# A dilated gated convolution on one core: the first window's loads reordered between queues, the last octet's gate and stores cut into halves and banks

## The chip, the cores and the metric

The kernel runs on 1 core of one Trainium2 chip. Its time is device microseconds of one execution. Five engines take part, each with its own instruction stream: PE (matmuls; its weight loads are listed as PEld), DVE (element-wise on SBUF and PSUM), ACT (element-wise and the tables for tanh and sigmoid), POOL (memsets, masks, and DMAs issued by software) and SP (which here only issues DMAs). DMAs issued by SP travel on queue q1, those issued by ACT on q10, those issued by POOL on q0; all three queues are served by the same 16 DMA engines.

## The reference

```
B, T, D, K = 2, 16000, 144, 15          # x [B,T,D], w [K,D,2D], w_o [D,D], all bf16
xp = pad(x, 28 rows of zeros ahead of each sequence)
h  = sum over i of  xp[:, 28 - 2*i : 28 - 2*i + T, :] @ w[i]
f, g = h[..., :D], h[..., D:]
out = (tanh(f) * sigmoid(g)) @ w_o
```

## The kernel before, in words

**Tiling.** Each sequence of 16000 rows is cut into windows of 2048 rows, 16 windows in all (the last of a sequence overlaps its neighbour, and only its last 104 of 128 row groups are stored). A window holds 16 row phases for 128 row groups; it is worked on as two octets (rho 0 and 1), one for the 8 even phases and one for the 8 odd ones, so there are 32 octets, n = 0 to 31.

**Channels.** 144 channels do not fit 128 partitions. The first 128 arrive by a transposing DMA of x (`load`, L89, tile xn). The other 16, the remainder, are gathered in 32-byte runs (`gather`, L99, tile xt), regrouped by residue on ACT (`rest`, L113) and differenced on DVE (`rest_diff`, L117) into xs, written back to a DRAM scratch xg (`spread`, L123; one DMA for each of the two), and read from there by two more transposing DMAs (`remainder`, L128, tiles rx and re).

**The convolution.** The 15 taps are folded in the manner of a fast convolution: differences of x (`d2`, `d4`, `d8`, `d48`, `d28`, `d24`, `d248`, all DVE at L160) meet sums of the weights. The weight sums are made once at the start: on DVE (`sm`, `ss`, `a1v`, `av`, `bc`, `ev`, L167) and on PE by an identity matrix with an eviction on ACT (`summed`, L235 and L237, called by `raw_sums`, `pair_sums`, `rest_sums`). w arrives in four quarters of its taps (L204); the 16 remainder rows of every tap arrive as `raw` (L206, L207). Each octet has leaves A1, A2, A3, B1, C1, E1 of matmuls into PSUM banks (L302), copies of them on ACT (L331, L335, L366) and combinations on DVE (L369, L387, L392) that end in y. Then tanh and sigmoid on ACT (L397), their product z on DVE (L404), a transposing DMA of z (L408), the output matmul (L434), its cast into the window's tile o (L424 on ACT, L426 on DVE), and one store of a whole window (L450, rows of 4608 bytes).

**What sets the order.** The schedule is manual: every engine runs its instructions in the order in which the program issues them. For octets in the middle this order comes from `PLAN` (L16): each entry is a step and the octet, relative to the running one, that it is done for. The start is written out by hand: fillers of zeros that keep PE busy (`NWARM` matmuls at L186, `keep` at L288), the loads, the weight sums, and the list `first` (L569) for octet 0. The step `wg` is `spread`, `cr` is `rest` and `dr` is `rest_diff`; at L578 those of window 1 are put early, in the place of `wg`, among the first steps of octet 1. The end is written out too: `finish_early` (L520) stands ahead of the product of the last octet's second gate, `finish` (L529) behind it. The last octet's z is transposed on PE (`z_by_pe`, L411) and not by DMA. Octets 29, 30 and 31 are called a, b and c below: a is the second of window 14, b and c are the two of window 15.

**The start before.** SP issues xn(0), w's first and second quarter, the two raw loads, w's third and fourth quarter, then the transposes rx(0), re(0), xn(1) and the gather xt(1). ACT issues xt(0) and the first of the two writes to xg, POOL issues the second one. SP waits, in order, for what each of its DMAs needs.

**The end before.** tanh and sigmoid of c are done as two gates of 576 columns each (k = 0 and 1). Window 15 is stored by two DMAs of whole rows when both b and c are cast: row groups 24 to 63 from SP, 64 to 127 from ACT.

Of the kernel before, what the change touches and what calls it, by code (L numbers as in the profile page):

```python
# [8 lines left out]
BF16 = mybir.dt.bfloat16  # L9
F32 = mybir.dt.float32  # L10
# [16 lines left out]
def kernel(  # L27
# [16 lines left out]
    NWARM = 20  # L44
# [88 lines left out]
    def derive_steps(s):  # L133
        ahead = {"x": 0}

        def sub(name, of, d, first=None, run=0):
# [4 lines left out]
            def go(which=slice(None)):  # L141
                if which.start in (None, 0):
                    s[name] = xd_pool.tile([P, WB], BF16, name=name)
                t, x = s[name], s[of]
                if name == "d4":
                    forms = [((0, [[1, hi]]), (4, [[4, hi // 2], [1, 2]]), (0, [[4, hi // 2], [1, 2]]))]
                elif first is None:
                    forms = [((0, [[1, hi]]), (d, [[1, hi]]), (0, [[1, hi]]))]
# [8 lines left out]
                for form in forms[which]:  # L157
                    o, a, b_ = (bass.AP(t_.tensor, t_[:, c + p:c + p + 1].offset, [t_.ap[0]] + dims)
                                for (c, dims), t_, p in zip(form, (t, x, x), [pad.get(k, 2) for k in (name, of, of)]))
                    nc.vector.tensor_tensor(out=o, in0=a, in1=b_, op=ALU.subtract)  # L160
# [38 lines left out]
    gather(0, nc.scalar)  # L199
# [48 lines left out]
    spread(0, (nc.scalar, nc.gpsimd))  # L248
# [17 lines left out]
    for c in range(4):  # L266
# [4 lines left out]
        if c == 2:  # L271
            pre0["d48"]()
# [72 lines left out]
    class Octet:  # L345
# [48 lines left out]
        def act(self, k, name, lo, func):  # L394
            t = act_pool.tile([P, 4, D], BF16, name=name)
            self.g[name, k] = t
            nc.scalar.activation(out=t[:], in_=self.t["y"][:, k::2, lo:lo + D], func=func)  # L397

        def mult(self, k, part):
            z = self.get(z_pool, "z", [P, 9, CM], BF16)  # L400
            o, lo, n = dict(a=(z[:, k:8:2, :], 0, CM), b=(z[:, 8, :].rearrange("p (r c) -> p r c", c=CR)[:, k::2, :], CM, CR),
                            z=(z[:].rearrange("p g c -> p (g c)").rearrange("p (r c) -> p r c", c=D)[:, k::2, :], 0, D))[part]
            th, sg = self.g["th", k], self.g["sg", k]
            nc.vector.tensor_tensor(out=o, in0=th[:, :, lo:lo + n], in1=sg[:, :, lo:lo + n], op=ALU.mult)  # L404
# [6 lines left out]
    def z_by_pe(o, blocks, by):  # L411

        zt, z = o.get(zt_pool, "zt", [P, 9, P], BF16), o.t["z"]
        for i in range(0, len(blocks), 4):
            b = blocks[i:i + 4]
            ps = bank(True)[:].bitcast(BF16).rearrange("p (g m) -> p g m", m=256)
            for k, g in enumerate(b):
                nc.tensor.transpose(ps[:, k, 0:P], z[:, g, :], ident[:])
            copy_by(by, zt[:, b[0]:b[-1] + 1:2, :], ps[:, 0:len(b), 0:P])
        o.zt = zt  # L420
# [7 lines left out]
    def outproj(o, g, end=False):  # L428
        r0, n = 3 * g, min(3, 8 - 3 * g)
        o.po[g] = bank(False) if end else ps_o.tile([P, 512], F32, name="po", tag="po")  # L430
        if not o.by_phase:
            for c in range(r0, r0 + n + 1):
                a, e = max(c - 1, r0), min(c + 1, r0 + n)
                nc.tensor.matmul(o.po[g][:, (a - r0) * D:(e - r0) * D], lhsT=o.zt[:, c, :],  # L434
                                 rhs=wo_z[:, c, a - c + 1:e - c + 1, :].rearrange("p r e -> p (r e)"), start=c == r0, stop=c == r0 + n,
                                 skip_group_check=True)
            return
        nc.tensor.matmul(o.po[g][:, 0:n * D], lhsT=o.zt[:, 8, :], rhs=wo_bd[:, r0:r0 + n, :].rearrange("p r e -> p (r e)"),  # L438
                         start=True, stop=False)
        for i in range(n):  # L440
            nc.tensor.matmul(o.po[g][:, i * D:(i + 1) * D], lhsT=o.zt[:, r0 + i, :], rhs=wo_m[:], start=False, stop=i == n - 1)  # L441
# [5 lines left out]
    def store(wi, eng, a=0, e=P):  # L447
        b, t0, m0 = wins[wi]
        a = max(a, m0)
        eng.dma_start(out=out[b, t0 + 16 * a:t0 + 16 * e, :].rearrange("(m r) e -> m r e", r=16), in_=outs[wi][a:e, :, :])  # L450
# [7 lines left out]
    def issue(n, name):  # L458
# [38 lines left out]
        elif name[:2] == "th":  # L497
            o.act(int(name[2]), "th", 0, ACT.Tanh)
# [120 lines left out]
```

## Time and profile before

| what | value |
|---|---|
| median of 3 runs | 332.78 us (331.69 to 332.83) |
| the profiled execution's own time | 332.82 us |
| its span in the trace | 330.8 us, so 2.0 us lie around it |
| PE busy | 321.4 us (97%) |
| DVE, ACT busy | 293.5 us (89%), 242.0 us (73%) |
| granted clock | 0.999 |
| last matmul of the convolution starts | 320.67 us |
| last store issued | 326.37 us |

The span is read in three stretches: the start, up to about 24 us, in which loads and waits set the pace; the middle, in which PE is busy nearly all the time; and the end from 320.7 us, in which there is no convolution left and a chain of small steps leads to the last byte stored. In the trace an idle time is shown in brackets with what ended it.

### The profile page before, as it was taken

What the parts mean: (1) busy time and instruction counts of PE and PEld (TensorE: products, weight loads), DVE (VectorE), ACT (ScalarE), POOL (GpSimd) and SP (SyncE); (2) the same over time, 40 slices, a digit from 0 to 9 for tenths busy, and PEclk for the clock granted to TensorE, in tenths of its full rate; (3) what the DMA queues carried; (4) which work ended last, traced back from release to release, by engine and by line L of the source; (5) the groups of instructions that cost most, each with busy time, mean ns of one, the idle gap of its engine ahead of it and who ended that gap; (6) DMA issues with size and microseconds to landing.
All of it is one profiled execution on the core that took longest, in us unless ns stands there. A gap on an engine that the chain in (4) does not pass through costs nothing.

```text
span 330.8 us, 7432 instructions
## 1 busy us (share of the span) xinstructions
PE 321.4 (97%) x2657; PEld 303.1 (92%) x2657; DVE 293.5 (89%) x664; ACT 242.0 (73%) x571; POOL 26.3 (8%) x56
## 2 busy tenths in 40 slices
PE   8899999999999999999999999999999999999993
PEld 3589999999999999999999999999999999999982
DVE  2889999989999998999999899999989999998683
ACT  2737777777877777788777778877777787777763
POOL 5959100000000000000000000000000000000000
PEclk9999999999999999999999999999999999999999
DMA  8779897895949579594979769495986859594113
GB/s 173 160 139 157 155 210 138 151 185 100 206 109 204 151 130 222 77 213 102 175 181 169 157 119 187 109 209 137 145 208 119 171 112 189 154 143 132 38 36 129
DMA packets 194993, 49.64 MB, mean 150 GB/s; under 512 B 190487, under 2 KB 192896, under 8 KB 194957
## 3 DMA queue, kind: packets, MB, share of 16 engines
q1 hardware_dynamic: 188894, 40.07, 69.6%
q10 hardware_dynamic: 4799, 8.58, 7.0%
q0 software_dynamic: 1264, 0.53, 0.9%
q8 instruction: 20, 0.33, 0.4%
q14 instruction: 16, 0.13, 0.1%
HBM read 2.82 MB, written 11.40 MB: 43 GB/s over the span
## 4 chain that ended last, share of the span: by engine, by line
PE 90%; DMA 4%; SPq 2%; DVE 2%; issue 1%; POOL 1%; ACT 0%; DVEq 0%
PE bc L302 56%; PE a L302 25%; PE po L434 9%; DMA xn<-in_x_dram 2%; DMA xt<-in_x_dram 1%; SPq L128 1%; DMA xg<-zero 1%; SPq L89 1%; DVE d L160 0%; DVE o L426 0%; DVE y L392 0%; DVE z L404 0%; POOL xg L123 0%; PE bc L438 0%; PE bc L441 0%
## 5 line engine op out<-in xcount | busy, mean ns | idle before, releaser
L302 PEld LDWEIGHTS <-d 128*128 128x128 bf16 x1792 | 225.4, 145 | 7.8 <-issue 1.4
L302 PE MATMUL bc<-w_all,d 128*128 128x288 bf16 x832 | 140.0, 286 | 0.3 <-DVE t L387 0.3
L392 DVE TENSOR_TENSOR y<-q,bc 128x288 f32<-128x288 f32 x192 | 86.4, 450 | 7.6 <-PE bc L302 5.7
L331 ACT COPY bc<-bc 128x288 f32<-128x288 f32 x97 | 38.5, 397 | 30.1 <-PE bc L302 24.3
L369 DVE TENSOR_TENSOR q<-a1s,a 128x288 f32<-128x288 f32 x126 | 54.2, 451 | 1.5 <-PE a L302 0.8
L424 ACT CAST o<-po 128x432 bf16<-128x432 f32 (+1 forms) x87 | 41.7, 479 | 17.1 <-PE po L434 17.1
L160 DVE TENSOR_TENSOR d<-d 128x516 bf16<-128x516 bf16 (+3 forms) x65 | 52.2, 805 | 0.0
L302 PE MATMUL a<-sm,d 128*128 128x288 bf16 x252 | 50.2, 286 | 0.0
L331 ACT COPY a<-a 128x288 f32<-128x288 f32 x95 | 36.6, 386 | 13.6 <-PE a L302 10.6
L160 DVE TENSOR_TENSOR d<-xn 128x516 bf16<-128x516 bf16 (+2 forms) x48 | 41.1, 859 | 5.1 <-DMA xn<-in_x_dram 5.1
L397 ACT ACTIVATE th<-y 128x576 bf16<-128x576 f32 x64 | 43.9, 685 | 1.1 <-DVE y L392 1.1
L397 ACT ACTIVATE sg<-y 128x576 bf16<-128x576 f32 x64 | 43.7, 683 | 0.0
L434 PE MATMUL po<-wo_z,zt 128*128 128x144 bf16 (+1 forms) x323 | 43.4, 253 | 0.0
L302 PE MATMUL bc<-bc,d 128*128 128x288 bf16 x256 | 41.8, 286 | 0.0
L302 PE MATMUL bc<-wo_p,re 128*128 128x288 bf16 x128 | 36.6, 286 | 0.0
L302 PE MATMUL bc<-we_r,re 128*128 128x288 bf16 x128 | 36.6, 286 | 0.0
L387 DVE TENSOR_TENSOR t<-q,bc 128x288 f32<-128x288 f32 x64 | 28.8, 451 | 8.3 <-PE bc L302 8.3
L434 PEld LDWEIGHTS <-zt 128*128 128x128 bf16 x341 | 29.9, 98 | 4.1
L335 ACT COPY bc<-bc 128x288 f32<-128x288 f32 x64 | 25.0, 393 | 11.2 <-PE bc L302 7.0
L392 DVE TENSOR_TENSOR y<-t,bc 128x288 f32<-128x288 f32 x64 | 26.1, 450 | 5.9 <-PE bc L302 5.9
L404 DVE TENSOR_TENSOR z<-th,sg 128x576 bf16<-128x576 bf16 (+1 forms) x66 | 29.1, 443 | 0.0
L302 PEld LDWEIGHTS <-re 128*128 128x128 bf16 x256 | 28.8, 113 | 0.0
(79 smaller groups left out, 275.5 us busy)
## 6 DMA issues: line engine op xcount, KB each, us to landing
out_dram<-o ACTq DMA_DIRECT2D x13, 576.0 KB
xg<-xs SPq DMA_DIRECT2D x30, 65.0 KB
xt<-in_x_dram SPq DMA_DIRECT2D x13, 71.5 KB
w_all<-in_w_dram SPq DMA_DIRECT2D x3, 288.0 KB
out_dram<-o SPq DMA_DIRECT2D x1, 576.0 KB
zt<-z SPq DMA_TRANSPOSE x31
out_dram<-o ACTq DMA_DIRECT2D x1, 468.0 KB
out_dram<-o ACTq DMA_DIRECT2D x1, 288.0 KB
```

The source lines that it names most:

```text
L89: nc.sync.dma_start_transpose(out=xn[:, lo:WB], in_=src)
L160: nc.vector.tensor_tensor(out=o, in0=a, in1=b_, op=ALU.subtract)
L302: nc.tensor.matmul(ps[:, 0:D2], lhsT=l, rhs=r, start=start, stop=stop, skip_group_check=on)
L331: nc.scalar.copy(out=self.ts[1][:, 0:D2], in_=self.ts[0][:, 0:D2])
L335: nc.scalar.copy(out=self.other[i][:, 0:D2], in_=self.ts[i][:, 0:D2])
L369: nc.vector.tensor_tensor(out=self.get(cp_pool, name, [P, 2, D2], F32)[:, i, :], in0=self.t["a1s"][:, i, :], in1=leaf.ts[i][:, 0:D2], op=op)
L387: nc.vector.tensor_tensor(out=self.get(cp_pool, "t3", [P, 2, D2], F32)[:, i, :], in0=self.t["q3"][:, i, :], in1=self.C1.ts[i][:, 0:D2], op ...
L392: nc.vector.tensor_tensor(out=y[:, k + 4 * i, :], in0=self.t[q][:, i, :], in1=ts[i][:, 0:D2], op=op)
L397: nc.scalar.activation(out=t[:], in_=self.t["y"][:, k::2, lo:lo + D], func=func)
L404: nc.vector.tensor_tensor(out=o, in0=th[:, :, lo:lo + n], in1=sg[:, :, lo:lo + n], op=ALU.mult)
L424: nc.scalar.copy(out=o, in_=a)
L434: nc.tensor.matmul(o.po[g][:, (a - r0) * D:(e - r0) * D], lhsT=o.zt[:, c, :], rhs=wo_z[:, c, a - c + 1:e - c + 1, :].rearrange("p r e -> p ...
```

## The change

It has three parts.

**The start's queues.** xt(0) is issued by SP right behind xn(0), not by ACT. The first write to xg goes to SP too, and stands ahead of the two raw loads and of w's last quarter; w's first three quarters stay ahead of it. SP's order becomes xn(0), xt(0), w in three quarters, xg, raw, raw, w's last quarter, rx(0), re(0), xn(1), xt(1).

**The start's sums.** NWARM falls from 20 to 18, and `keep` from 8 fillers in all to 3. On DVE d2 moves between the first and the second sums, d48 from behind the third to behind the second, and d24, which was done in two halves, is one instruction; d28 comes ahead of the sum bc. On PE the pair sums come in an order that follows w's quarters, and the common part of A3 (`vA3`) comes ahead of A2's private part. `rest` and `rest_diff` of window 1 move behind the step q2_1 of octet 1, with `spread`.

**The end.** c's second gate is done in two halves, k = 1 and k = 3, of 288 columns. `finish_early` and `finish` become one function; c's z is transposed as [0, 2, 4, 6], [1, 5] and [3, 7, 8]; its output matmuls are ordered by when their block arrives. b's half of window 15 is stored as soon as b is cast, and each of c's three banks by a DMA of its own: all of these write runs of 288 bytes, 832 runs for b, 312, 312 and 208 for c.

```diff
-    NWARM = 20
+    NWARM = 18
...
-                    if name == "d24" and s is sets[0]:
-                        forms = [((first, runs), (first, runs), (first + e, runs)), ((first + e, runs), (first + 2 * e, runs), (first + e, runs))]
-                    else:
-                        forms = [[(c, [runs[0], [k, 2], runs[1]]) for c, k in ((first, e), (first, 2 * e), (first + e, 0))]]
+                    form = [(c, [runs[0], [k, 2], runs[1]]) for c, k in ((first, e), (first, 2 * e), (first + e, 0))]
...
-    gather(0, nc.scalar)
+    gather(0)
...
-    for c in range(0, 16, 4):
+
+    def load_w(c):
         nc.sync.dma_start(out=w_all[:, c:min(c + 4, K), :], in_=w[c:min(c + 4, K), 0:CM, :].rearrange("k c d -> c k d"))
-        if c == 4:
-            nc.sync.dma_start(out=raw[:, 0, :], in_=w[0:K:2, CM:D, :])
-            nc.sync.dma_start(out=raw[0:P - CR, 1, :], in_=w[1:K:2, CM:D, :])
+    for c in (0, 4, 8):
+        load_w(c)
...
-    spread(0, (nc.scalar, nc.gpsimd))
+    spread(0, (nc.sync, nc.gpsimd))
+    nc.sync.dma_start(out=raw[:, 0, :], in_=w[0:K:2, CM:D, :])
+    nc.sync.dma_start(out=raw[0:P - CR, 1, :], in_=w[1:K:2, CM:D, :])
+    load_w(12)
...
-        if c == 2:
-            pre0["d48"]()
+        if c < 2:
+            pre0[("d2", "d48")[c]]()
...
+    pair_sums(0)
     raw_sums(0)
+    pair_sums(1)
     rest_sums(slice(0, 3))
-    pair_sums(0)
-    pair_sums(1)
-    keep(5)
-    raw_sums(1, (1,))
+    keep(2)
+    raw_sums(1)
     add(av[:], quad[:, :, 0], quad[:, :, 1])
-    pre0["d2"]()
+    pre0["d28"]()
     add(bc[:, 2:4], wq[:, 2:4, 0], wq[:, 2:4, 1])
-    pre0["d28"]()
-    pre0["d24"](slice(0, 1))
+    pre0["d24"]()
...
+    def outproj_last(o, blocks):
+
+        for c in blocks:
+            g, lo, n, w_ = (c // 3, c % 3, 1, wo_m[:]) if c < 8 else \
+                (c - 8, 0, min(3, 8 - 3 * (c - 8)), wo_bd[:, 3 * c - 24:min(3 * c - 21, 8), :].rearrange("p r e -> p (r e)"))
+            new = g not in o.po
+            if new:
+                o.po[g] = bank(False) if g else ps_o.tile([P, 512], F32, name="po", tag="po")
+            nc.tensor.matmul(o.po[g][:, lo * D:(lo + n) * D], lhsT=o.t["zt"][:, o.at[min(c, 8)], :], rhs=w_, start=new, stop=c >= 8,
+                             skip_group_check=True)
...
+    def store_phases(o, wi, r0, n, eng):
+        b, t0, a = wins[wi]
+        r = o.rho + 2 * r0
+        dst = bass.AP(out.tensor, out[b, t0 + 16 * a + r, 0:1].offset, [[16 * D, P - a], [2 * D, n], [1, D]])
+        eng.dma_start(out=dst, in_=outs[wi][a:P, r:r + 2 * n - 1:2, :])
...
-    def finish_early():
-
-        n = NO - 3
-        for g in range(3):
-            outproj(live[n], g, g > 0)
-        for g, by in ((0, "DVE"), (1, "DVE"), (2, "ACT")):
-            project_out(live[n], window_out(n), g, by)
-        z_by_pe(live[NO - 1], [0, 2, 4, 6], "ACT")
-
...
+        a, b, c = (live[n] for n in range(NO - 3, NO))
+        c.at = {}
+        window_out(NO - 1)
+        for g in range(3):
+            outproj(a, g, g > 0)
+        outproj(b, 0, True)
+        z_by_pe(c, [0, 2, 4, 6], "ACT")
+        c.mult(1, 4)
+        c.mult(3, 4)
+        for g, by in ((0, "ACT"), (1, "DVE"), (2, "DVE")):
+            project_out(a, outs[NW - 2], g, by)
         store(NW - 2, nc.sync)
...
+        for g in (1, 2):
+            outproj(b, g, True)
+        z_by_pe(c, [1, 5], "ACT")
+        z_by_pe(c, [3, 7, 8], "DVE")
+        for g, by in ((0, "DVE"), (1, "ACT"), (2, "ACT")):
+            project_out(b, outs[NW - 1], g, by)
+        store_phases(b, NW - 1, 0, 8, nc.sync)
+        outproj_last(c, [0, 2, 4, 1, 5, 6, 8, 3, 9, 7, 10])
+        for g, by, eng in ((0, "ACT", nc.sync), (1, "DVE", nc.sync), (2, "ACT", nc.scalar)):
+            project_out(c, outs[NW - 1], g, by)
+            store_phases(c, NW - 1, 3 * g, min(3, 8 - 3 * g), eng)
...
-    first = ["vA1", "kA1", lambda: raw_sums(1, (0,)), lambda: keep(1), "pA1_0", "pA1_1", "a1s_0", "a1s_1", "vA2", "kA2", lambda: keep(2), "vB",
-             "kB", "pA2_0", "q2_0", "pA2_1", "q2_1", "vA3", "kA3", "pB_0", "dB_0", "pB_1", "dB_1", lambda: pre0["d24"](slice(1, 2)), "pA3_0",
-             "q3_0", "pA3_1", "B2_0", "q3_1", "B2_1", evs, "yB2_0", pre0["d248"]]
+    first = ["vA1", "kA1", lambda: keep(1), "pA1_0", "pA1_1", "a1s_0", "a1s_1", "vA2", "kA2", "vB", "kB", "vA3", "kA3", "pA2_0", "q2_0",
+             "pA2_1", "q2_1", "pB_0", "dB_0", "pB_1", "dB_1", "pA3_0", "q3_0", "pA3_1", "B2_0", "q3_1", "B2_1", evs, "yB2_0", pre0["d248"]]
...
-    todo = sorted((2 + at_wg[0], False, at_wg[1] - .5, n, name) if n == 2 and name in ("cr", "dr") else
+    todo = sorted((1, False, behind + .1 * "cr dr wg".split().index(name), n, name) if n == 2 and name in ("cr", "dr", "wg") else
...
+    last = {"th1": lambda: live[NO - 1].act(1, 4), "sg1": lambda: live[NO - 1].act(3, 4), "m1": finish}
```

More of the change, by code (lines that the diff above doesn't have):

```diff
@@ L413, in z_by_pe @@
         zt, z = o.get(zt_pool, "zt", [P, 9, P], BF16), o.t["z"]
[L414 to L420, printed above, removed]
+        ps = bank(True)[:].bitcast(BF16).rearrange("p (g m) -> p g m", m=256)
+        n = len(o.at)
+        for k, g in enumerate(blocks):
+            o.at[g] = n + k
+            nc.tensor.transpose(ps[:, k, 0:P], z[:, g, :], ident[:])
+        copy_by(by, zt[:, n:n + len(blocks), :], ps[:, 0:len(blocks), 0:P])
     def copy_by(by, o, a):
@@ L430, in outproj @@
         o.po[g] = bank(False) if end else ps_o.tile([P, 512], F32, name="po", tag="po")
[L431 to L441, printed above, removed]
+        for c in range(r0, r0 + n + 1):
+            a, e = max(c - 1, r0), min(c + 1, r0 + n)
+            nc.tensor.matmul(o.po[g][:, (a - r0) * D:(e - r0) * D], lhsT=o.zt[:, c, :],
+                             rhs=wo_z[:, c, a - c + 1:e - c + 1, :].rearrange("p r e -> p (r e)"), start=c == r0, stop=c == r0 + n,
+                             skip_group_check=True)
[7 more added lines that the diff above has]
+            nc.tensor.matmul(o.po[g][:, lo * D:(lo + n) * D], lhsT=o.t["zt"][:, o.at[min(c, 8)], :], rhs=w_, start=new, stop=c >= 8,
+                             skip_group_check=True)
     def project_out(o, ob, g, by="ACT"):
@@ L497, in issue @@
         elif name[:2] == "th":
-            o.act(int(name[2]), "th", 0, ACT.Tanh)
+            o.gate(int(name[2]), "th", 0, ACT.Tanh)
         elif name[:2] == "sg":
-            o.act(int(name[2]), "sg", D, ACT.Sigmoid)
+            o.gate(int(name[2]), "sg", D, ACT.Sigmoid)
         elif name[0] == "m":
-            for part in "ab" if o.by_phase else "z":
-                o.mult(int(name[1]), part)
+            o.mult(int(name[1]))
         elif name == "zt":
@@ L548 @@
     outwards = {"g0", "g1", "g2", "po0", "po1", "po2", "ost"}
-    at_wg = next((at, i) for i, (name, at) in enumerate(plan) if name == "wg")
+    behind = next(i for i, (name, at) in enumerate(plan) if name == "q2_1")
     def weights_out():
@@ L585 @@
             continue
-        if (n, name) in gates:
-            gates.clear()
-            finish_early()
-        issue(n, name)
-    finish()
+        if n == NO - 1 and name in last:
+            last[name]()
+        else:
+            issue(n, name)
 _INS = ['x', 'w', 'w_o']
```

62 lines of the change are left out of this document (25 added, 37 removed).

## The prediction

> **What bounds the kernel now.** The page first: PE is busy 97% of the span, so the middle is PE's own work, which the change leaves alone; time can only come from places where PE has nothing to do. The table of stretches says where those are: PE is busy 5.00 of 5 us from 25 to 30, but 4.36, 4.94, 4.30 and 4.34 of 5 us in the four stretches from 5 to 25.
>
> ```profile
> PE 321.4 (97%) x2657; PEld 303.1 (92%) x2657; DVE 293.5 (89%) x664; ACT 242.0 (73%) x571; POOL 26.3 (8%) x56
> ...
> 15.00:20.00 5.00, 4.30 (x32) 3.70 (x31) 4.34 (x10) 1.89 (x6) 1.36 (x3) 1.00 1.12 228
> 20.00:25.00 5.00, 4.34 (x35) 4.06 (x34) 4.14 (x9) 2.27 (x7) 4.62 (x10) 1.00 0.50 59
> 25.00:30.00 5.00, 5.00 (x43) 4.92 (x42) 5.00 (x14) 3.45 (x8) 5.00 (x11) 1.00 0.99 163
> ```
>
> The timeline of the first 25 us (start, duration, engine, what, and in brackets the idle time before it and its releaser) names the waits.
>
> ```profile
> 6.24 1.15 DVE L160 TENSOR_TENSOR d<-xn 128x516 bf16<-128x516 bf16 x2 [5.08 <-DMA xn<-in_x_dram]
> ...
> 11.64 2.12 SPq L128 DMA_TRANSPOSE rx<-xg  x1
> ...
> 13.11 0.41 PE L302 MATMUL a<-a1v,xn 128*128 128x288 bf16 x2
> ...
> 16.63 0.31 PE L302 MATMUL bc<-ns_r,rx 128*128 128x288 bf16 x1 [0.66 <-DMA rx<-xg]
> ...
> 22.84 0.32 DVE L117 TENSOR_TENSOR xs<-xt 104x320 bf16<-104x320 bf16 x1 [0.86 <-DMA xt<-in_x_dram]
> ...
> 23.58 0.41 PE L302 MATMUL bc<-ev,d 128*128 128x288 bf16 x2 [0.66 <-DVE y L392]
> ```
>
> The reader is to see two stalls with one root. rx is issued only at 11.64, because its input, the write to xg, lands late; PE waits for rx at 16.63. Behind rx on SP come re, xn(1) and xt(1), so xt(1) is late as well: DVE stands 0.86 us for it at 22.84, the y behind it is late, and PE waits 0.66 us for that y at 23.58. From there on PE is full.
>
> The DMA view in small windows tells why xg is late (packets, MB, share of 16 engines; half a microsecond from 4.5, then quarters from 7.25, 10.5 and 324.5):
>
> ```profile
> q10 hardware_dynamic: 630, 0.02, 70.9%
> q1 hardware_dynamic: 238, 0.06, 61.5%
> ...
> q1 hardware_dynamic: 136, 0.08, 109.6%
> ...
> q10 hardware_dynamic: 178, 0.03, 62.0%
> ...
> q1 hardware_dynamic: 23, 0.11, 100.7%
> ```
>
> q10 carries xt while xn is still running on q1, and ACT's write to xg, issued at 7.20, moves only at 9.75 to 11.0, when w on q1 is nearly through. Share x 16 engines x window / packets gives ns per packet: 9.0 for xt's 32-byte runs, 13.9 for xg's 160 bytes, 32 for w's 576, 175 for the 4608-byte rows of the store.
>
> At the end the chain is gate, product, transposes, casts, store:
>
> ```profile
> 321.91 0.68 ACT L397 ACTIVATE th<-y 128x576 bf16<-128x576 f32 x1 [0.80 <-DVE y L392]
> ...
> 323.20 0.53 DVE L404 TENSOR_TENSOR z<-th,sg 128x512 bf16<-128x512 bf16 x2
> ...
> 324.12 0.56 DVE L426 COPY zt<-a 128x512 bf16<-128x512 bf16 x2 [0.39 <-PE a L418]
> ...
> 326.37 0.55 ACTq L450 DMA_DIRECT2D out_dram<-o  x1
> ```
>
> Bytes of the last stores move from 327.0 to 329.05, and the span ends at 330.8.
>
> **The start, step by step.** *xt on q1.* Alone, transposes ran at 548 to 565 packets per half microsecond (rx, 13.5 to 15.0) against 400 to 436 beside xt. xn has 2048 packets: its data end at about 4.3 instead of 4.9, and DVE's first step, 1.3 us behind the data as now, starts at 5.6 instead of 6.24. xt follows: 2288 packets at 907 per half microsecond (xt(1), 20.5 to 21.0), so data end at 5.6 against 5.4 now; with a lag between 1.3 (xt(0)) and 1.6 us (xt(1)) ACT's copy starts at 6.9 to 7.2 (6.71 now).
>
> *w.* Its first three quarters then take about 0.95 us each (512 packets, 136 per quarter microsecond): data end at 6.5, 7.5 and 8.45, usable 1.1 us later (as now: 7.5 to 8.58), so 7.6, 8.6, 9.6. The third comes 0.8 us earlier than now, since raw no longer stands ahead of it.
>
> *xg.* SP reaches this write at about 4.6 and waits for ACT's copy until 7.5; behind it stand raw (issues of 0.79 and 0.83 us), w's last quarter, rx, re, xn(1), xt(1), so this wait is the new lock of the queue. On q1 the write comes right behind w's third quarter: 416 x 13.9 / 16 = 0.4 us, done at 8.85 instead of 11.0. rx is issued when SP is through raw and w, 7.85 + 0.79 + 0.83 + 0.4 = 9.9, and xg has landed, about 9.9: 10.0 instead of 11.64. With rx's own 5.0 us from issue to use it lands at 15.0.
>
> *The price.* w's last quarter, issued at 9.5, has its data at 10.25 to 11.0 and is usable at 12.2. DVE by then: 5.6 + d8, d4 1.15; xs 0.31 from 7.0; the first sums at 7.65 (0.76 with ss), d2 1.24, second sums 1.05, d48 0.69, third sums 0.76: 11.95. It waits 0.25 us, then third and last sums and a1v end at 13.3 (12.85 now). PE's first convolution matmul moves from 13.11 to 13.35: **0.24 us lost**. The seven fillers dropped (0.21 us each once warm) stand in waits on both sides and I count them at nothing; without that cover they would be worth 1.5 us.
>
> *Then.* A1 and its copies as now, 0.24 later; A2's private part starts when ACT has copied it, at 15.85 by ACT's row of 0.4 us copies, and rx is there. It ends at 16.6 (17.32 now). With vA3 already done, pB (4 x 0.12) and pA3 (0.73) end at 17.85, where they end at 18.82 now. d24 in one piece ends at 16.45 and hides in that time. From there to 22.92 PE has 4.1 us of work: 21.95. Is y there? DVE: q2 to 17.3, q3 to 18.4, ev 0.45, y 0.45, d248 0.65, d2(1) 1.24 (xn(1), issued at 14.4 instead of 16.30, is in by 19.3), y: 21.45. So xs no longer ends last, and PE goes on at 21.95 instead of 23.58: **1.6 us gained**. What is late next is y again, with 0.5 us in hand.
>
> *Moved later.* `rest`, `rest_diff`, `spread` of window 1: 0.46 us on ACT, 0.32 on DVE, two issues on SP. They go behind q2_1, about 24.5, so rx(1) is issued at about 25.9 (25.67 now) and lands near 30.5 to 31; PE needs it at 33.50 - 1.6 = 31.9. Cover 1 us, thin; without it each 0.1 us late is 0.1 us. xn(2), last in that row, lands near 37.2 with d2 wanting it at 37.0: a DVE wait of some 0.2 us, which 89% busy can hide.
>
> Bounds for the start: it could lose 0.2 (only the later w counts) or gain 2.1 (DVE's y moves from 23.53 to 21.45). I take 1.6.
>
> **The end, step by step.** ACT stands idle 0.80 us before c's second gate, waiting for y of k = 3. In halves, k = 1 runs in that gap; a half is a 288-column ACT row (0.39 to 0.41 us, 0.30 apart), so k = 3 ends at 321.91 + 0.30 + 0.39 = 322.6 instead of 323.17. Products: 322.95 instead of 323.73. But DVE now casts two banks of a (0.60 and 0.45) behind them, ahead of the copy of zt: that copy starts at 323.85 (324.12 now) and ends at 324.3 (324.68). PE has only five matmuls left behind it: 0.6 us, not 1.17. The casts of c end at about 325.8 (326.33 now). Half a microsecond is won there, and the stores decide what is left of it. a's store is issued later (a's first bank waits on ACT for the evens' copy): 324.0 against 323.48; its rows take 1.5 us as now and end at 326.25. Behind it on q1 come b and two banks of c, on q10 the third: 832 + 624 + 208 = 1664 packets of 288 bytes. Between 13.9 ns (160 bytes) and 32 ns (576 bytes) a straight line gives 19 ns: 1664 x 19 / 16 = 2.0 us. Data end at 328.25 instead of 329.05: **0.8 us gained**. Bounds: 1.8 gained (if nothing queues: last issue 326.1 + 0.77 + 0.36), or 5.0 lost at 75 ns a packet, which q0 shows for short rows of w_o around 25.5. The line is nearest in size, queue and kind.
>
> The Trainium skill, DMA: Bandwidth & Descriptors, Specifications, gives 512 bytes as the least size for full rate and says that a write below it is read, modified and written. The 160-byte writes to xg at 13.9 ns show no such step on this trace; the rival below prices it.
>
> **Sum.** 332.8 - 1.6 - 0.8 = **330.4 us**, against the profiled execution's 332.82, which is the median (332.78) to 0.04.
>
> **Rivals.**
> *Short stores dear.* Mechanism: 288-byte runs into out_dram, 104 packets per engine behind a. At 40 ns: 4.2 us, data end at 330.4, tail +1.35, total 332.6. It overtakes the start's gain from 42 ns and is slower by over 0.5% from 58 ns; at 75 ns, 336.2. For it: q0's rows. Against it: xg's. 0.13, of which 0.08 slower.
> *The lock.* xt lands later, or raw's issues stretch, and w's last quarter with them; every microsecond behind 12.2 is one behind the start. One late: 331.4. For it: w's packets took 40 to 88 ns at 5.5 to 6.25 and 8.0 to 9.25. 0.16.
> *DVE swallows it.* DVE is busy 5.00 of 5 us from 25 to 30, and takes in xs there; PE then waits for y later and the start's gain is gone: 332.0. Against it: DVE gains 2.1 us, more than PE. 0.08.
> *The clock.* The first fillers, from 1.22 to about 5.0, take 0.43 us each and the later ones 0.21; with seven fewer, waits for w may halve PE's rate once more, and for the same 3.8 us that costs 1.9: 332.3. The trace shows PE gaps of 0.66 us without it. The Trainium skill, TensorE: Matmul & The Clock Gate, Part 1, has the gate close after an idle window of about 3.4 us; by that rule no gap here is long enough. 0.04.
> The forecast has 0.56; 0.03 is left for what I do not see.
>
> Within 0.5% (1.66 us) is about what a measurement of this kernel can tell from no change, so faster means below 331.1: the forecast and 0.02 of the lock, 0.58; same: the rest of the lock, DVE, the clock, the milder stores and 0.01 of the unseen, 0.32; slower: dear stores and the other 0.02 of the unseen, 0.10. The range takes in the lock and stores at 40 ns above, and part of the bounds' gains below: 329.0 to 332.6.
>
> **What would show it.** Right: DVE's first step near 5.6; rx issued near 10.0; no PE wait for rx; PE's first ev matmul near 21.95; window 1's rx without a wait; the store's last bytes near 328.2, with packets near 19 ns. Wrong: PE's first convolution matmul behind 14; a wait for y or rx(1) between 22 and 40; q1 packets of the last stores above 40 ns.

## The result and the profile after

| what | before | after |
|---|---|---|
| median of 16 runs each, same chip | 332.46 us | 333.59 us |
| ratio after / before, 95% interval | | 1.0038 [1.0026, 1.005] |
| profiled execution's own time, its span | 332.82, 330.8 us | 333.56, 331.7 us |
| span's start to PE's first ev matmul | 23.58 | 21.92 |
| from there to PE's last convolution matmul | 297.09 | 298.49 |
| from there to the end of the span | 10.13 | 11.29 |

The changed kernel is slower by 0.4%, where 330.4 us and faster had been predicted; 333.59 lies above the range. The last three rows add up to the span. They are called **start**, **middle** and **end** below, and every run is read by them: the start gained 1.66 us, the middle lost 1.40, the end lost 1.16.

Page of the changed kernel, busy time by engine, then its table of stretches (length, then busy time and instructions of PE, PEld, DVE, ACT, POOL, then clock, DMA share, GB/s):

```profile
PE 319.4 (96%) x2650; PEld 302.3 (91%) x2650; DVE 293.6 (89%) x664; ACT 242.1 (73%) x574; POOL 26.3 (8%) x56
```

```profile
15.00:20.00 5.00, 4.89 (x41) 4.68 (x40) 4.63 (x10) 2.25 (x7) 1.03 (x3) 1.00 1.08 206
20.00:25.00 5.00, 5.00 (x43) 4.94 (x42) 4.85 (x11) 2.93 (x9) 5.00 (x11) 1.00 0.29 40
25.00:30.00 5.00, 5.00 (x43) 4.93 (x42) 5.00 (x12) 4.31 (x10) 5.00 (x10) 1.00 0.84 113
30.00:35.00 5.00, 3.61 (x29) 3.18 (x28) 3.96 (x11) 1.29 (x5) 2.50 (x6) 1.00 1.24 249
```

The last of these stretches in the kernel before:

```profile
30.00:35.00 5.00, 5.00 (x42) 4.84 (x41) 5.00 (x12) 2.86 (x8) 3.12 (x7) 1.00 1.28 196
```

PE, which stood idle in the stretches from 15 to 25, is now nearly full there (4.89 and 5.00 of 5 us); the hole is behind them, 1.39 us in the stretch from 30 to 35, where before was full. The timeline of the same execution names it:

```profile
5.09 1.15 DVE L155 TENSOR_TENSOR d<-xn 128x516 bf16<-128x516 bf16 x2 [3.92 <-DMA xn<-in_x_dram]
...
10.44 2.07 SPq L128 DMA_TRANSPOSE rx<-xg  x1
...
13.55 0.41 PE L300 MATMUL a<-a1v,xn 128*128 128x288 bf16 x2
...
16.26 0.28 PE L300 MATMUL bc<-ns_r,rx 128*128 128x288 bf16 x1
...
21.92 0.41 PE L300 MATMUL bc<-ev,d 128*128 128x288 bf16 x2
...
26.06 3.43 SPq L128 DMA_TRANSPOSE rx<-xg  x1
...
33.31 0.31 PE L300 MATMUL a<-ns_r,rx 128*128 128x288 bf16 x1 [1.25 <-DMA rx<-xg]
```

The first window's rx is issued at 10.44 instead of 11.64, PE does not wait for it, and the ev matmul stands at 21.92. But window 1's rx, called rx(1) below, is issued at 26.06 and PE stands 1.25 us for it. The kernel before had issued it at 25.67 and used it, without a wait, at 33.50:

```profile
25.67 2.29 SPq L128 DMA_TRANSPOSE rx<-xg  x1
...
33.50 0.29 PE L302 MATMUL a<-ns_r,rx 128*128 128x288 bf16 x1
```

The end in the same timeline:

```profile
322.08 0.44 ACT L399 ACTIVATE th<-y 128x288 bf16<-128x288 f32 x1 [0.57 <-DVE z L409]
...
324.22 0.38 SPq L458 DMA_DIRECT2D out_dram<-o  x1
...
324.99 2.97 SPq L464 DMA_DIRECT2D out_dram<-o  x3
...
325.29 0.40 ACT L428 CAST o<-bc 128x288 bf16<-128x288 f32 x1
325.72 0.35 ACTq L464 DMA_DIRECT2D out_dram<-o  x1
```

c's last cast ends 5.31 us behind the last convolution matmul (5.66 before), so the compute chain did get shorter; but SP issues short-run stores from 324.99 to 327.96, and the last packet of the stores ends at 329.77, 9.36 us behind the last convolution matmul. Before it ended at 329.51, 8.84 behind it: the 329.05 of the prediction leaves out the last packets, two of which start at 329.19. So 0.5 us of the end's loss lie ahead of the last byte. The other 0.7 lie behind it: from the last packet to the end of the span it is 1.95 us here and 1.25 before. The gate of k = 3 waits for a product on DVE, not for y.

### The profile page after: what moved, and what is told of

The parts are those of the page before. It is cut to its first block, busy times and chain, and to the rows that moved or that the text cites. A ratio compares the mean times of both kernels' runs of the same rounds, so it can differ in the third digit from the quotient of the medians.

```text
span 331.7 us, 7425 instructions
## 1 busy us (share of the span) xinstructions
PE 319.4 (96%) x2650; PEld 302.3 (91%) x2650; DVE 293.6 (89%) x664; ACT 242.1 (73%) x574; POOL 26.3 (8%) x56
## 4 chain that ended last, share of the span: by engine, by line
PE 87%; POOL 4%; DMA 3%; issue 2%; DVE 1%; ACT 0%; SPq 0%; ACTq 0%; POOLq 0%
PE bc L300 53%; PE a L300 24%; PE po L437 9%; DMA rx<-xg 2%; DMA xt<-in_x_dram 1%; POOL wo_z L573 1%; POOL wo_z L571 1%; POOL wo_z L565 1%; POOL xg L252 1%; SPq L89 0%; POOL wo_bd L566 0%; POOL xg L123 0%; PE po L449 0%; DVE o L430 0%; DVE z L409 0%
## 5 line engine op out<-in xcount | busy, mean ns | idle before, releaser
L428 ACT CAST o<-po 128x432 bf16<-128x432 f32 (+1 forms) x89 | 42.7, 479 | 17.1 <-PE po L437 17.0
L155 DVE TENSOR_TENSOR d<-d 128x1032 bf16<-128x1032 bf16 (+1 forms) x64 | 52.1, 814 | 0.0
L329 ACT COPY a<-a 128x288 f32<-128x288 f32 x95 | 36.7, 386 | 12.4 <-PE a L300 9.4
L399 ACT ACTIVATE th<-y 128x576 bf16<-128x576 f32 (+1 forms) x65 | 44.2, 679 | 0.9 <-DVE z L409 0.6
L399 ACT ACTIVATE sg<-y 128x576 bf16<-128x576 f32 (+1 forms) x65 | 43.9, 675 | 0.0
L409 DVE TENSOR_TENSOR z<-th,sg 128x576 bf16<-128x576 bf16 (+2 forms) x68 | 29.2, 434 | 0.6 <-ACT sg L399 0.6
```

The lines of the kernel that those rows point to most:

```text
L329: nc.scalar.copy(out=self.ts[1][:, 0:D2], in_=self.ts[0][:, 0:D2])
L399: nc.scalar.activation(out=t[:], in_=self.t["y"][:, k::step, lo:lo + D], func=func)
L428: nc.scalar.copy(out=o, in_=a)
```

## The experiments

The theory after the result: the start does what was predicted; its gain is lost to rx(1), which was moved later; the short-run stores cost more than the shorter chain saves. Rivals: the start's gain is one execution's; the loss in the middle comes from DVE; the end's loss comes from the new order of gates and casts.

All fourteen, and before and after, by the three parts of their profiled executions. "Time" is the median less the median of before on the same chip beside it (332.46 us for after, 331.69 to 331.94 for the others).

| kernel | start | middle | PE's wait for rx(1) | end | time | ratio [95%] |
|---|---|---|---|---|---|---|
| before | 23.58 | 297.09 | none | 10.13 | | |
| b_copy | 22.91 | 297.10 | none | 10.09 | +0.34 | 1.0007 [0.9989, 1.0024] |
| after | 21.92 | 298.49 | 1.25 | 11.29 | +1.13 | 1.0038 [1.0026, 1.005] |
| a_copy | 21.69 | 298.15 | 0.74 | 11.36 | +1.60 | 1.0056 [1.0042, 1.0069] |
| a_wg_early | 21.87 | 296.84 | none | 11.29 | +0.76 | 1.0019 [1.0004, 1.0033] |
| a_row_stores | 21.74 | 298.19 | 0.91 | 9.77 | −0.15 | 1.000 [0.9988, 1.0012] |
| a_old_end | 21.70 | 298.22 | 1.08 | 10.08 | +0.51 | 1.0016 [1.0003, 1.0028] |
| b_new_end | 22.39 | 297.09 | none | 11.42 | +1.24 | 1.0041 [1.0027, 1.0055] |
| a_xt_behind_rx | 21.95 | 299.45 | 0.88 | 11.30 | +2.53 | 1.0075 [1.0054, 1.0096] |
| a_wo_early | 21.76 | 297.76 | 0.17 | 11.18 | +0.97 | 1.0028 [1.0012, 1.0044] |
| a_no_wo | 22.06 | 297.07 | none | 11.27 | +0.20 | 1.0012 [0.9994, 1.0029] |
| a_no_wo_xt | 22.00 | 297.07 | none | 11.43 | +1.07 | 1.0032 [1.0014, 1.005] |
| a_96_only | 22.05 | 297.73 | 0.48 | 10.32 | +0.77 | 1.003 [1.0017, 1.0043] |
| b_short_runs | 22.63 | 297.09 | none | 11.58 | +0.89 | 1.0028 [1.0011, 1.0046] |
| wg_early_rows | 21.78 | 296.70 | none | 9.82 | −1.59 | 0.9949 [0.9931, 0.9966] |
| wg_early_rows_gate | 22.02 | 296.83 | none | 9.25 | −1.55 | 0.9958 [0.9944, 0.9973] |

### The halves of the change apart

a_wg_early puts the three steps of window 1 back:

```
-    behind = next(i for i, (name, at) in enumerate(plan) if name == "q2_1")
+    at_wg = next((at, i) for i, (name, at) in enumerate(plan) if name == "wg")
...
-    todo = sorted((1, False, behind + .1 * "cr dr wg".split().index(name), n, name) if n == 2 and name in ("cr", "dr", "wg") else
+    todo = sorted((2 + at_wg[0], False, at_wg[1] - .5, n, name) if n == 2 and name in ("cr", "dr") else
```

> The changed kernel with one thing put back: rest, rest_diff and spread of window 1 stand again among the first steps of octet 1, as before. Theory of place: the PE wait of 1.25 us for rx(1) at 32 us is there because the spread of window 1 now stands behind q2_1 of octet 1, so that rx(1) is issued at 26.1 while its first use came 1.7 us earlier. Then rx(1) is issued before 25, the wait for it is gone or under 0.2 us, PE may wait up to 0.4 us for a y behind xs instead, and the time is 332.2 to 332.6. Rival of transport: rx(1) takes 7.2 us from issue to use whatever its place, because it runs beside the loads of w_o; then the wait stays at 1 us or more and the time stays within 0.3 us of 333.56.

rx(1) is issued at 24.15 and nobody waits for it. The middle is 1.31 to 1.65 us shorter than in the two profiles of the changed kernel, and DVE takes xs(1) in at 20.87 without a wait. The move was not needed, and it is what cost the middle. In time less of it shows: a_wg_early is 0.76 us over before, where the theory had it below, and so only 0.37 to 0.84 us under the changed kernel and a_copy, with intervals that overlap or nearly meet. The same edit on top of row stores, further down, is worth 1.44 us in time (−0.15 to −1.59).

a_row_stores stores window 15 in two DMAs of whole rows again, behind the new chain:

```
...
-        store_phases(b, NW - 1, 0, 8, nc.sync)
...
-            store_phases(c, NW - 1, 3 * g, min(3, 8 - 3 * g), eng)
+        store(NW - 1, nc.sync, 0, P // 2)
+        store(NW - 1, nc.scalar, P // 2)
```

> The changed kernel with window 15 stored again by two DMAs of whole 4608-byte rows when b and c are cast; gates in halves, transposes and casts as changed. Theory of run length: the four stores of 288-byte runs hold the end up (last bytes at 329.75, though the casts end at 325.72). Then the row stores are issued at 325.8, their bytes end near 328.5, and the time is 332.1 to 332.5. Rival of the chain: what is late is a's store, issued 0.74 us later than before, and everything behind it; then whole rows end no earlier than 329.4 and the time stays at 333.2 to 333.6.

The end falls from 11.3 to 9.77, which is 0.36 below before's 10.13: gates, transposes and casts of the new end save a third of a microsecond, and the short-run stores cost 1.5. The last bytes come at 328.48, as the theory had it (328.5). The time falls by 1.3 us against the changed kernel (1.75 against a_copy), to 0.15 us below before, where 0.3 to 0.7 below had been expected.

a_old_end has the changed start with before's end (the functions of the end as in the diff's minus lines), b_new_end the old start with the changed end:

```
 # a_old_end, at the end of the program
-    last = {"th1": lambda: live[NO - 1].act(1, 4), "sg1": lambda: live[NO - 1].act(3, 4), "m1": finish}
+    gates = [(NO - 1, "m1")]
...
+    finish()
```

> The changed start and sums with the end of the kernel before (one gate of 576 columns, finish_early and finish, two stores of whole rows). If start and end add up, the convolution ends 0.26 us earlier than before and the end takes its old 10.1 us from the last convolution matmul: 332.3 to 332.6, 0.2 to 0.3 us under before. If the new end had hidden a dearer start, this is slower than before.

> The start of the kernel before with the changed end alone. If start and end add up, the end takes 11.3 us from the last convolution matmul instead of 10.1: 333.5 to 334.0, 1.0 to 1.3 us over before. A rival in which the end's loss comes from the changed start (queues, semaphores carried along) gives before's time within 0.3 us.

Both crossings show the same prices: the end is 10.08 with the old code and 11.42 with the new, whatever the start. But a_old_end came out 0.5 us *over* before, not below: its start is only about 0.7 us earlier than the one that b_new_end shows on this chip for the old code, 22.39 and not 23.58, and its middle is 1.13 us longer than before's.

### Is 23.58 one execution's?

b_copy is the kernel before, unchanged, and a_copy (below) the changed one; neither has an edit.

> The kernel before, unchanged, to have a second profile of its start. The theory (the stalls in the profile shown of before, 0.66 us for rx and 0.66 us for y, belong to that one execution, in which rx was issued at 11.64): here the first matmul with ev starts at 22.0 to 22.6, not at 23.58, and PE waits for rx(0) or for y by less than 0.3 us each. Rival (the stalls are in each execution of before, and what was seen with the changed end came from another layout): ev at 23.3 to 23.8 again. Ratio to before 1.000, within 0.15%.

In between. In the timeline of b_copy PE waits 0.25 us for rx (0.66 in the profile of before), and still 0.63 for y:

```profile
15.99 0.31 PE L302 MATMUL bc<-ns_r,rx 128*128 128x288 bf16 x1 [0.25 <-DMA rx<-xg]
...
22.17 0.33 DVE L117 TENSOR_TENSOR xs<-xt 104x320 bf16<-104x320 bf16 x1 [0.96 <-DMA xt<-in_x_dram]
...
22.91 0.40 PE L302 MATMUL bc<-ev,d 128*128 128x288 bf16 x2 [0.63 <-DVE y L392]
```

Four profiles of the old start have ev at 23.58, 22.91, 22.39 and 22.63, mean 22.88. Twelve of the changed start have it between 21.69 and 22.06, mean 21.88. So the late xt(1) is in the old code, and its size differs from one execution to the next; the changed start takes out that spread and **1.0 us** on average, not the 1.6 of the profile that the prediction had. The spans say the same of that profile: beside the experiments, on three chips, before ran 95 times with spans from 329.0 to 330.6 us (medians 329.8 to 329.9), and the profile that the prediction was made from has 330.8. Whether that is the execution or its chip, no run here tells.

### Why rx(1) takes seven microseconds

Three causes stood against each other: the gather xt(2), which is ahead of rx(1) in q1; the loads of w_o on q0, which POOL issues from 19.6 to 33; and slow patches that come anyway. a_xt_behind_rx issues the gather behind rx(1) by one more key in `todo`; a_wo_early drops the copy that holds POOL's loads back:

```
+                  (2, False, [p[0] for p in plan].index("rx") + .5, n, name) if n == 4 and name == "xt" else
...
-        held = const.tile([1, 1], BF16)
-        nc.gpsimd.tensor_copy(out=held[:], in_=ev[0:1, 0, 0:1])
```

> The changed kernel; only the gather xt(2), which stands right ahead of rx(1) on SP, is issued behind rx(1). Theory 1 (the wait for rx(1) is rx(1) queued in q1 behind the 2288 short packets of xt(2), 1.2 to 1.7 us of them): rx(1) is issued at 25.6 to 25.9, lands in 5.0 to 5.7 us, PE's wait for it falls from 0.9 to 1.25 us to 0 to 0.3 us, and the time is 0.7 to 1.1 us below that of the changed kernel, which is 1.3 to 1.7 us over before on this pair of chips: 0.3 to 0.9 us over before (ratio 1.001 to 1.0027). Theory 2 (what counts is the place of rest, rest_diff and the write to xg, so that rx(1) is asked for too late whatever stands ahead of it): the wait stays at 0.8 us or more and the ratio at 1.004 or above. Theory 3 (transport is slow from 26 to 30 since the loads of w_o run then): in between, the wait 0.5 to 0.9.

> The changed kernel without the copy on POOL that holds POOL's two loads of w_o back until ev is there: they are issued at about 15.5 and end by 29 instead of 32. No result changes. Theory 3 (rx(1) is late because w_o's short packets share the 16 engines with it): PE's wait for rx(1) falls by half or more, and the ratio to before comes down by 0.0015 or more, unless rx(0) or xt(1) are now late by the same packets. Theory 1 (xt(2) ahead in q1): the wait for rx(1) stays within 0.3 us of the 0.9 to 1.25 us seen, ratio 1.004 to 1.0055.

The trace also has sixteen landing marks for each of these transposes; where PE waited for rx(1), the last mark stands 0.04 to 0.05 us ahead of the matmul. So the time from issue to landing can be read in every profile, also where nobody waited.

The queue theory fell. With nothing ahead of it rx(1) still takes 6.99 us from issue to landing (7.21 in the changed kernel), and re, now behind the gather, is issued over 4.74 us; the transpose of z behind it is late, and PE waits a second time:

```profile
25.95 2.41 SPq L128 DMA_TRANSPOSE rx<-xg  x1
28.41 0.54 SPq L99 DMA_DIRECT2D xt<-in_x_dram  x1
29.05 4.74 SPq L128 DMA_TRANSPOSE re<-xg  x1
...
32.98 0.31 PE L300 MATMUL a<-ns_r,rx 128*128 128x288 bf16 x1 [0.88 <-DMA rx<-xg]
...
40.95 0.54 PE L437 MATMUL po<-wo_z,zt 128*128 128x144 bf16 x4 [1.28 <-DMA zt<-z]
```

a_wo_early, whose loads begin at 15.4, 4.2 us sooner, has 0.17 us of the wait left, and rx(1) lands after 5.96 us. In time this is unclear: its ratio is 0.001 below the changed kernel's and 0.0028 below a_copy's, where theory 3 asked for 0.0015. Whether it is the loads of w_o was then asked directly, by leaving them out:

```
-        for g in range(9):
-            if g:
-                nc.gpsimd.dma_start(out=wo_z[0:CR * g, g, 0, :], in_=w_o[D - CR * g:D, :])
...
+        nc.gpsimd.memset(wo_m[:], 0.0)
```

> The changed kernel without any load of w_o (its tiles are zeros, so the output is zeros). Theory w_o (its loads beside rx(1) slow it): rx(1) takes at most 5.8 us from issue to use, PE's wait for it is 0 to 0.2 us, and the time is 0.6 to 1.0 us below the changed kernel's +1.1 to +1.6 over before. Rival (rx(1) is slow by itself, 1.5 to 2 us behind xt(2) in its queue, then its own 2048 packets with a slow patch in them): 6.5 us or more, wait 0.5 to 1.2 us, and the time as the changed kernel's.

> As a_no_wo, and the gather xt(2) is issued behind rx(1). Theory w_o: no wait for rx(1), as in a_no_wo. Rival queue (xt(2) ahead of it counts once w_o is out of the way): rx(1) at 4.5 to 5.2 us from issue to landing, no wait here, though there is one in a_no_wo. Rival patch (slow patches come whatever else is in the queues): a wait of 0.5 us or more in both. The time may be higher than a_no_wo's by up to 1.3 us, since re and the transpose of z behind the gather were late by that much when it was moved alone.

In the timeline of a_no_wo rx(1) is issued as late as in the changed kernel and is there at 32.06 without a wait:

```profile
26.21 3.06 SPq L128 DMA_TRANSPOSE rx<-xg  x1
...
32.06 0.29 PE L300 MATMUL a<-ns_r,rx 128*128 128x288 bf16 x1
```

The middle is 297.07, as before's. Issue to landing of rx(1), in us:

| loads of w_o | profiles | rx(1) |
|---|---|---|
| left out | a_no_wo, a_no_wo_xt | 5.19, 5.17 |
| begun at 15.4 | a_wo_early | 5.96 |
| as in both kernels, spread of window 1 late | after, a_copy, a_row_stores, a_old_end, a_xt_behind_rx, a_96_only | 6.43 to 7.21 |
| as in both kernels, spread of window 1 early | before, b_copy, b_new_end, b_short_runs, a_wg_early, wg_early_rows, wg_early_rows_gate | 5.86 to 7.72 |

It is the loads of w_o: both kernels without them have the shortest times and no wait, with the gather ahead of rx(1) or behind it. How the loads slow it is not shown. The packets of q1 do not simply fall where q0 has many: in half microseconds of the changed kernel q1 moves 262 packets beside 26 on q0 (29.5 to 30) and 257 beside 2 (29.0 to 29.5), and in the kernel before 470 beside 47 (29.5 to 30). In a_no_wo it moves 317 and then 564 in these two stretches. What makes the dip that is left at 29.0 to 29.5 is open.

a_no_wo_xt is 0.9 us over a_no_wo in time with the same three parts to 0.2. Its profiled execution, with a span of 330.5, is one of its shortest: over all ten the median span is 330.85, against 330.2 for a_no_wo. So most of the longer time is in the span, if not in that of the profiled execution; where it arises is open.

### The price of short runs

a_96_only leaves out the last 8 of 104 row groups; b_short_runs gives before's own end the short runs, b's from SP, c's from ACT.

```
-        eng.dma_start(out=dst, in_=outs[wi][a:P, r:r + 2 * n - 1:2, :])
+        eng.dma_start(out=dst, in_=outs[wi][a:a + 96, r:r + 2 * n - 1:2, :])
```

```
-        store(NW - 1, nc.sync, 0, P // 2)
-        store(NW - 1, nc.scalar, P // 2)
+        b, t0, m0 = wins[NW - 1]
+        for rho, eng in ((0, nc.sync), (1, nc.scalar)):
+            dst = bass.AP(out.tensor, out[b, t0 + 16 * m0 + rho, 0:1].offset, [[16 * D, P - m0], [2 * D, 8], [1, D]])
+            eng.dma_start(out=dst, in_=outs[NW - 1][m0:P, rho:16:2, :])
```

> The changed kernel with the last 8 of the 104 row groups of window 15 left unstored, so that each DMA of short runs has 96 rows instead of 104 and 1536 packets instead of 1664; the output lacks those rows. Theory 1 (the 104 rows go to 13 of the 16 engines, 128 packets each at about 24 ns, 3.1 us; 96 rows go to all 16, 96 packets each, 2.3 us): the last bytes come 0.6 to 0.9 us earlier against the last cast, the share of the 16 engines in the last stores rises from at most 93% to above 100%, and the time is 0.5 to 0.9 us below that of the changed kernel in this call. Theory 2 (the short writes have one common rate, however many engines carry them): 8% less, 0.2 to 0.3 us. Theory 3 (the three stores' issues on SP, 2.97 us in a row, set the end, and they go by rows or not at all): 0 to 0.2 us.

> The kernel before; only the two stores of window 15 differ: the even phases (b) go from SP when b is cast, the odd phases (c) from ACT when c is cast, each as 832 runs of 288 bytes in place of rows of 4608. The casts stay where they are. Theory 1 (13 engines, about 24 ns a run): b's bytes start near 326.2, c's near 327.1, and 1664 x 24 / 13 = 3.1 us after the start they end at 329.3, that is 0.1 to 0.4 us over before (ratio 1.0003 to 1.0012), though half of the bytes start 0.8 us earlier. Theory 2 (the prediction's 16 engines at 19 ns, 2.0 us): last bytes at 328.1 to 328.3, 0.7 to 0.9 us below before (ratio 0.9973 to 0.9979). Theory 3 (the new end's cost is in its four issues on SP, not in the runs): as theory 2, since SP issues one.

> The changed kernel itself, to have a second profile of it and a time beside the other three. Ratio 1.003 to 1.005. If the account so far is right, its profile has the first matmul with ev at 21.7 to 22.0, a PE wait of 0.8 to 1.3 us for rx(1), and 11.2 to 11.5 us from the last convolution matmul to the end of the span. Rival (the wait for rx(1) is one execution's and comes and goes): no wait or under 0.3 us.

The DMA view from 326 to 328, a_copy first, then a_96_only; the last cast ends at 325.13 and 325.06:

```profile
DMA packets 1165, 0.33 MB, mean 165 GB/s; under 512 B 1164, under 2 KB 1164, under 8 KB 1165
q1 hardware_dynamic: 953, 0.27, 65.1%
q10 hardware_dynamic: 212, 0.06, 12.3%
```

```profile
DMA packets 1519, 0.42 MB, mean 209 GB/s; under 512 B 1519, under 2 KB 1519, under 8 KB 1519
q1 hardware_dynamic: 1311, 0.36, 84.0%
q10 hardware_dynamic: 208, 0.06, 12.1%
```

In these 2 us the packets' time is 77.4% of 16 engines' with 104 rows (12.4 of 16) and 96.1% with 96 (15.4), at 21.3 and 20.2 ns a packet. A share does not count engines, though: from 327 to 328 alone a_copy has 95%. Two other counts of the trace are plainer. a_copy's four stores are followed by 52 packets of 4 bytes, 13 for each, a_96_only's by 64, 16 for each; in before it is 10 for the store of 40 rows and 16 for the one of 64. And over the whole of the stores a_copy moves 1664 runs in 3.08 us, 540 a microsecond, a_96_only 1536 in 2.26 us, 679 a microsecond: 1.26 times as many, where 16/13 is 1.23. The mean packet is 23.0 ns in the one and 20.7 in the other. So the number of rows sets the rate, and by these counts mostly through the number of engines. The end falls by 1.04 us and the time by 0.83, where theory 1 gave 0.5 to 0.9 for the time and the others at most 0.3; its share above 100% did not come. The Trainium skill, DMA: Bandwidth & Descriptors, section on why a DMA increments its semaphore by 16, has the rule: the largest number up to 16 that divides the slowest dimension of both sides; for 104 that is 13, for 96 it is 16. The 13 and 16 packets of 4 bytes agree.

b_short_runs came out at +0.89 us with an end of 11.58, worse than theory 1's 0.1 to 0.4 (the others had a gain). 797 of b's 832 packets start within 1.5 us, from 325.75 to 327.25, as theory 1 has it (832 x 24 / 13 = 1.5); the rest trail to 327.9. But c's bytes start 7.36 us behind the last convolution matmul, at 327.08, where it had 327.1 − 320.67 = 6.4. That 6.4 belongs to SP's rows; in before ACT's rows start 6.98 behind it. The other 0.4 us go with a longer issue, which the theory had not:

```profile
324.16 0.95 SPq L546 DMA_DIRECT2D out_dram<-o  x1
...
325.42 1.01 ACTq L546 DMA_DIRECT2D out_dram<-o  x1
```

832 runs take 0.95 and 1.01 us to issue, where rows took 0.55 at ACT, and nothing else stands in SP's way here. With two issues of short runs the end is about as late as with the changed kernel's four, so the number of issues is not shown to cost anything.

### Both costs out

wg_early_rows is the changed kernel with the edits of a_wg_early and of a_row_stores together.

> The changed kernel with both disputed parts undone: rest, rest_diff and the writes of xg of window 1 back at their old place, and the last window stored in whole rows, when both of its halves are cast. If the two costs are separate and add up (0.77 us from before's start to the changed start without the move of window 1's steps; 0.33 us from the shorter end with row stores): 1.0 to 1.2 us below before, ratio 0.9964 to 0.9970. Rival (they do not add: the start's gain is swallowed on the way by DVE): 0.3 to 0.4 us below before, ratio 0.999; then the last matmul of the convolution starts no earlier than in the changed kernel. Rival (the changed start does not gain at all beyond one execution): ratio 1.000 or more.

> The version with both disputed parts undone (1.6 us below before, 0.9949), and the halves of c's second gate in buffers of their own, so that the half of k = 3 does not wait for the product of k = 0 to free one. Theory (that wait holds the gate back by 0.44 us, and with it the products, transposes, casts and the store): a further 0.3 to 0.45 us, ratio 0.9936 to 0.9941, and the time from the last convolution matmul to the end of the span falls from 9.8 to 9.4 us. Rival (the gate is not last: DVE's casts of a stand ahead of the copy of zt anyway): 0 to 0.1 us.

With window 1's steps at their old place and whole-row stores, the kernel is 1.59 us below before, ratio 0.9949 [0.9931, 0.9966]; expected were 1.0 to 1.2. By parts: start 22.88 − 21.78 = 1.1, middle 0.39, end 0.31, together 1.8. Why the middle is 0.25 to 0.4 shorter than before's in all three kernels with the old place was not followed.

wg_early_rows_gate gives the two halves of the second gate tiles of their own:

```
-            t = self.g[name, k] = act_pool.tile([P, 8 // step, D], BF16, name=name)
+            t = self.g[name, k] = act_pool.tile([P, 8 // step, D], BF16, name=name + ("h" if step == 4 else ""))
```

In its timeline the tanh of k = 3 no longer waits (its line in the changed kernel carried 0.57 for DVE's z), and the gates end 1.95 us behind the last convolution matmul instead of 2.45:

```profile
319.20 0.43 ACT L399 ACTIVATE thh<-y 128x288 bf16<-128x288 f32 x1
...
320.02 0.44 ACT L399 ACTIVATE thh<-y 128x288 bf16<-128x288 f32 x1
```

The end falls to 9.25, 0.57 less. In time this is not to be told from wg_early_rows: the intervals overlap, and the profiled start was 0.24 later in this run. The spans of all executions have medians of 328.0 us here and 328.3 there, where before has 329.8 beside both.

## Why the prediction was wrong, step by step

**The start: right in the changed kernel, measured from a late base.** The first step of DVE was given at 5.6 and came at 5.09, rx issued at 10.0 (10.44), the first convolution matmul at 13.35 (13.55), the ev matmul at 21.95 (21.92), without a wait for rx. That the last of these fits to 0.03 is in part luck: DVE began 0.5 us early, rx was issued 0.4 late, and its first matmul started at 16.26 where 15.85 was forecast. "1.6 us gained" held against the one execution that it was made from; over four profiles of the old start the gain is 1.0.

**"Moved later": the step that failed first.** It had rx(1) issued at 25.9 (26.06), landed "near 30.5 to 31" (33.27), and "Cover 1 us, thin". It was used at 33.31 with a wait of 1.25 us. The time to landing was taken from rx(0)'s 5.0 us; beside w_o's loads rx(1) takes 5.9 to 7.7 in thirteen profiles, 7.21 in this one, and 5.2 only where these loads are left out. Before, this was hidden: issued at 25.67 and needed only at 33.50, rx(1) had 7.8 us and took 5.95; in b_copy it took 7.38 of 7.9. PE's gain drew the need forward to 32.06 and the change put the issue back. The page of before had a row against it: the prediction itself quotes w_o's packets at 75 ns around 25.5, and uses them for the stores alone. By parts, this step cost 1.06 to 1.40 us in the two profiles of the changed kernel, all of the start's gain.

**The end, the compute chain: right in kind, half in size.** Gates were to end 322.6 − 320.67 = 1.93 us behind the last convolution matmul. They end at 2.45, since the tanh of k = 3 needs a buffer that DVE's product of k = 0 frees; with own buffers it is 1.95. The last cast was to come at 325.8 − 320.67 = 5.13, came at 5.31, and at 4.82 without that wait. The same wait makes a's store late: it was to be issued 324.0 − 320.67 = 3.33 us behind the last convolution matmul, came at 3.81, and at 3.32 with own buffers. The wait that takes the place of the one removed was a buffer, which none of the rivals named.

**"1664 x 19 / 16 = 2.0 us": the term mis-sized.** The 1664 packets move from 326.70 to 329.77, which is 3.1 us; the term is 1.1 too short. The packet was nearly right, 23 ns on average; what the sum had wrong is the 16 engines: with 13, as the rows of 104 have it, 1664 x 23 / 13 gives 2.9. The stretch also starts 0.7 us late, 6.29 behind the last convolution matmul instead of 326.25 − 320.67 = 5.58, since a's store was issued late and its rows took 1.7 us instead of 1.5. So bytes ended 9.36 us behind it and not 328.25 − 320.67 = 7.58. The end of the span also follows the last byte at 1.95 us and not at before's 1.25; why is open. The sum had most of that by luck, since its 329.05 for before's last byte made the distance 1.75. "0.8 us gained" became 1.16 lost. The rival of dear stores had the right sign and the wrong mechanism: it asked for 40 ns a packet.

**The other rivals.** The lock of SP's queue did not come (last quarter of w used at 12.38 with 0.26 us of wait, as forecast), nor did DVE swallow the gain. The granted clock was 0.99 or more in each run.

The sum as it is: 332.8 − 1.7 + 1.4 + 1.2 = 333.7 against 333.56 for the two profiled executions, and about −1.0 + 1.2 + 1.2 = +1.4 by means of the profiles, between the +1.13 and +1.60 measured.

## What to carry to other kernels

A transfer that runs "without a wait" shows only that its cover was long enough: before you move its issue later or its reader earlier, take its time from its own issue, beside its own neighbours on the DMA engines, and not from a sister transfer in another stretch. Look at the number of rows of a DMA as well as at the bytes of its runs: eight rows fewer of 104 made the rate of these stores 1.26 times as high. And a gain worked out from stalls of one profiled execution is only as firm as these stalls; a second profile of the same kernel here took 0.7 us off them.

## What the runs showed of the hardware

- rx(1) took 5.2 us from issue to landing without the loads of w_o on q0 and 5.9 to 7.7 us with them at their old place.
- Writes of 288 bytes to DRAM took 19 to 24 ns each on the average of a queue's stores, next to 13.9 ns for 160 bytes in the profile of before.
- A store of 104 rows is followed by 13 packets of 4 bytes, one of 96, 64 or 128 rows by 16, one of 40 rows by 10; with 96 rows for 104 the 288-byte runs moved at 679 a microsecond instead of 540.
- A store of 832 short runs kept SP 0.95 us and ACT 1.01 us with its issue; one of whole rows kept ACT 0.55 us.
- From the last packet of the stores to the end of the span it was 1.25 us with whole rows and 1.9 to 2.1 us with runs of 288 bytes.
